# A fused attention and maxout-FFN kernel: token tiles grouped 2, 2, 4, 4, 4, 4, 4 in place of 4, 2, 2, 4, 4, 4, 4, with every engine's order of work written anew

## The chip, the cores and the metric

The kernel runs on one core of a Trainium2 chip. The metric is the device time of one execution in microseconds; the kernel before is given as the median of three runs. Beside it there is one profiled execution, whose trace gives every instruction's start and duration. The engines go by the profile's names: PE (matrix multiplications; PEld is its loading of weights), DVE (vector engine), ACT (activation engine), POOL (GpSimd) and SP (here the engine that issues nearly all DMAs).

## The reference

Causal attention with 8 global and 96 local keys, and a linear bias per head, over 4 batches, 8 heads, 768 positions of 64 dimensions. Its output, as 3072 tokens of 512 features, goes through a feed-forward layer whose hidden value is the maximum of three products.

```
scores = scale * (q @ k.T) - slope[h] * dist        # dist: i - j for local keys, 96 for global ones
a      = softmax(where(keep, scores, -1e9))          # keep: the 8 first keys, or 0 <= i - j < 96
x      = (a @ v) -> [3072, 512]
h      = max(max(x @ w1, x @ w2), x @ w3)            # [3072, 768]
out    = h @ w_out                                   # [3072, 512], float32
```

## The kernel before

**Tiles.** The 3072 tokens are 24 tiles of 128, six per batch. For a tile T the kernel multiplies its queries with the keys of the tile and of the tile before it, into whose first columns the global keys have been copied (`u_S`, on PE, two halves g of four heads each), takes the exponential (`u_e`, ACT), multiplies with a mask that holds the bias (`u_m`, DVE; a few tiles get the bias by a matmul, `u_b`, and no mask), multiplies with the values (`u_A`, PE) and normalises (`u_n`, DVE), which leaves the tile's 128x512 attention output `xb`. That is transposed to `xT`, by PE and a copy (`u_t`, `u_u`) or by a DMA transpose that SP issues (`u_Z`).

**Chunks.** The feed-forward layer works on chunks of tiles, by the list `SIZES`. A chunk of four tiles makes matmuls 512 columns wide, one of two tiles 256 wide. `u_F` makes a unit of hidden features: chunk c, block f of 128 of the 768 hidden features, product j of the three; four matmuls into one PSUM bank. `u_f` empties that bank: for j = 0 a copy by ACT or DVE into a buffer `h01`, for j = 1 a maximum on DVE into the same buffer, for j = 2 a maximum on DVE into `ht`. When all six blocks of a chunk are there, `u_O` multiplies with `w_out`, six matmuls to a tile, `u_o` copies the bank to `staging`, `u_s` writes it to memory.

**Loads.** SP issues all loads: q, k and v for pairs of tiles (group G is the tiles 2G and 2G + 1; `u_l`, 512 KB each; the first four tiles' q and k come as one quadruple, group 12), the three weights in two pieces each (`u_w`: blocks f = 0, 1, which are 512 KB, and blocks f = 2 to 5, which are 1 MB), and `w_out` in three pieces (`u_q`). What has landed is float32 and is cast to bfloat16 by ACT, DVE or POOL (`u_c`, `u_v`, `u_W`, `u_Q`); a cast on POOL is made in two halves. q and k of a pair are transposed to `qkT` by PE (`u_x`, `u_y`), or from tile 10 on by two DMA transposes (`u_X`). In weight casts `w123_0`, `w123_1`, `w123_2` hold the blocks f = 0, 1, f = 2, 3 and f = 4, 5 of all three weights.

**Order.** Nothing is scheduled by a program: the string `SCHEDULE` lists the units, and each engine runs its instructions in that order. A unit reads `F1.5.0@7`: function `u_F`, chunk 1, block 5, product 0, buffer slot 7 of its ring. `RINGS` gives the number of slots; for PSUM there are eight banks. An engine that waits holds up all that stands behind it in its list; an instruction that writes a slot waits until the slot's last reader is done. SP waits the same way: a load waits for its slot, a DMA transpose for the `xb` or the casts that it reads, and each DMA for the eighth before it.

**The end.** `u_E` makes the output of the last chunk: tiles 0 and 1, tile 2, then tile 3 in pieces of 256, 128 and 128 columns. After it the table has one tile that was kept back, tile 0 of chunk 5, whose output is stored in two halves.

Of the kernel before, what the change touches and what calls it, by code (L numbers as in the profile page):

```python
# [24 lines left out]
    l0.12.1@0 l1.12.1@1 D10.512@0 l1.12.3@2 l0.12.2@3 l0.12.3@4 R K7 K6 B1.1 K4 B2.1 K2 B3.0 K1 K5 B0.1 B6.1  # L25
    K0 c0.12.3.2@0 l1.12.2@5 c0.12.1.1 B4.1 B5.1 c1.12.1.1@1 K3 x12.0.1@0 y0.0.1.0@0 B7.1 l2.0.2@0 D3.256@1
    x12.1.1@1 b0.1@2 v1.0.2 l2.1.2@1 c1.12.3.1 v1.1.2 b1.0@4 y0.1.1.0 b1.1@6 S1.1.1 l0.2.2@6 c0.12.2.1
    y1.0.1.1@1 y1.1.1.0 x12.0.2@0 e1.1@0 c1.12.2.1 x12.0.3 y0.0.0.1 l1.2.2@0 y1.0.0.1 x12.1.3@1 x12.1.2
    y0.1.0.0 S0.1.1 e0.1@1 G0.1 b2.1@6 v2.0.2 v3.0.2 w1.0@0 S1.0.1 G1.0 e1.0@2 b2.0@2 w0.0@0 y1.1.0.1 S2.1.1
    w1.1@1 S0.0.0@0 e0.0@3 l2.2.2@2 S2.0.1 v0.0.1 e2.0@4 w0.1@1 v0.1.1 m0.0.1 e2.1@5 v2.1.2 b3.0@4 A1@0  # L30
    V1.1.1 V1.0.2 G2.1 v3.1.2 w0.2@2 A0@2 S3.0.1 e3.0@6 b3.1@6 n1@0 c0.2.2.2@2 S3.1.1 G3.0 A2@0 V2.0.2
    e3.1@7 V2.1.2 n0@1 t0@2 W0.0.2 c1.2.2.1 u0.0@0 x2.1.2@3 y2.1.2.0@2 w1.2@2 x2.0.2@2 A3@4 t1@6 u1.0 n2@2
    y2.0.2.1 t2@7 n3@3 l0.3.2@1 l1.3.2@2 S4.1.0@0 V3.1.2 e4.1@0 V3.0.2 S4.0.0@2 W1.1.2 u2.1 t3@6 G4.1 u3.0
    W2.0.1 S5.1.0@4 e5.1@2 S5.0.0@0 e5.0@1 m4.1.1 W1.0.1 e4.0@3 F0.5.0@7 F0.4.0@6 W2.1.0 F0.3.0@4 f0.3.0.0@0
    F0.2.0@5 f0.4.0.1@1 F0.1.0@6 v4.1.2 v4.0.2 l2.3.2@0 f0.1.0.0@2 q2@0 v5.1.0 F0.0.0@0 F0.5.1@1 F0.4.1@4
    F0.2.1@6 m4.0.1 f0.0.0.0@3 v5.0.0 f0.5.0.0@4 m5.1.1 A4@2 V4.1.0 F0.3.1@0 W0.1.2 f0.4.1.1 W0.2.0 m5.0.1
# [54 lines left out]

LAST_BANKS = (6, 7, 3, 0, 1, 4, 5, 2)

LAST_STAGES = (8, 2, 0, 10, 11, 7, 6, 3, 4, 9, 1, 5)


@with_exitstack
def kernel(
# [13 lines left out]
    nc = tc.nc  # L112
# [366 lines left out]
    def u_E(slot):  # L479
# [12 lines left out]
        for tt, p in enumerate(po):  # L492
            f2_mm(p, last, tt, range(NF - 1))
# [118 lines left out]
```

## Time and profile before

| | us |
|---|---|
| median of 3 runs | 176.49 |
| lowest and highest | 175.44 and 176.92 |
| profiled execution, span from the first to the last instruction | 174.8 |
| first feed-forward matmul starts | 21.58 |
| last matmul ends | 171.2 |

The page gives no time of its own for the profiled execution beside its span; the median of the runs lies 1.7 us above that span. A row of a group reads: line, engine, operation, what it writes from what it reads, sizes, count, then busy time, mean duration of one in ns, and the idle time before them with what ended it. Matmuls overlap in the array: a 512-column matmul is shown as lasting 379 ns but the next one starts after some 216 ns, so that the pace is read from the chain of waits, which gives a stretch of matmuls with its length and count.

### The profile page before, as it was taken

To read this page: it belongs to the slowest core of one execution; us is meant where nothing else is said; L and a number is where in the kernel's file an instruction comes from. 1 tells how busy PE (TensorE), PEld (TensorE's weight loads), DVE (VectorE), ACT (ScalarE), POOL (GpSimd) and SP (SyncE) were. 2 spreads that over 40 slices of the span, in tenths; PEclk is the share of its full clock that TensorE was granted. 3 is DMA by queue.
4 is the path that set the end of the run, shared out by engine and by line. 5 is a ranking of instruction groups with operands and counts; after the bars stand their busy time and mean duration, and the time that the engine had idled before them with its cause. 6 is when DMAs were issued, how large, how long until landed. Compare 5 with 4: busy or idle time off the path is not lost.

```text
span 174.8 us, 3865 instructions
## 1 busy us (share of the span) xinstructions
PE 165.9 (95%) x1485; PEld 93.6 (54%) x1507; DVE 131.9 (75%) x268; ACT 95.4 (55%) x147; POOL 54.7 (31%) x99
## 2 busy tenths in 40 slices
PE   7997999999999999898999999999999999999991
PEld 2555745577676877544445545544445554444460
DVE  7889864988599897989898678899578993074910
ACT  5988897672868788440667688200345651402051
POOL 4049295057586717003730003240530000000000
PEclk9999999999999999999999999999999999999998
DMA  5999999999899899999996759998990046370035
GB/s 149 352 292 327 402 360 385 270 371 311 229 303 179 139 183 266 267 290 284 165 135 112 114 145 306 305 210 260 231 213 20 0 120 137 121 286 4 0 119 185
DMA packets 66403, 37.36 MB, mean 214 GB/s; under 512 B 24144, under 2 KB 61392, under 8 KB 66384
## 3 DMA queue, kind: packets, MB, share of 16 engines
q1 hardware_dynamic: 66240, 37.04, 83.3%
q8 instruction: 12, 0.20, 0.5%
q10 hardware_dynamic: 144, 0.07, 0.1%
q14 instruction: 7, 0.06, 0.1%
HBM read 25.17 MB, written 6.29 MB: 180 GB/s over the span
## 4 chain that ended last, share of the span: by engine, by line
PE 76%; DVE 10%; DMA 6%; ACT 3%; issue 2%; SPq 0%; DVEq 0%
PE psum L433 44%; PE psum L457 17%; PE psum L349 6%; DMA xT<-xb 3%; DMA rawqk<-in_k_dram 3%; DVE P L365 3%; PE psum L391 3%; PE psum L394 2%; PE psum L276 2%; DVE ht L452 1%; DVE xb L403 1%; ACT P L356 1%; PE psum L270 1%; DVE qb L195 1%; PE psum L335 1%
## 5 line engine op out<-in xcount | busy, mean ns | idle before, releaser
L433 PE MATMUL psum<-xT,w 128*128 128x512 bf16 (+1 forms) x491 | 97.5, 348 | 1.5 <-DMA xT<-xb 0.7
L433 PEld LDWEIGHTS <-w 128*128 128x128 bf16 x504 | 47.6, 98 | 42.9 <-DMA xT<-xb 0.9
L356 ACT ACTIVATE P<-psum 128x1024 bf16<-128x1024 f32 (+1 forms) x48 | 43.3, 954 | 10.4 <-PE psum L349 10.3
L449 DVE TENSOR_TENSOR h<-h,psum 128x512 bf16<-128x512 bf16 (+1 forms) x42 | 25.0, 605 | 15.9 <-PE psum L433 12.4
L457 PE MATMUL psum<-wo,ht 128*128 128x512 bf16 (+2 forms) x147 | 33.4, 362 | 0.5
L447 ACT CAST h<-psum 128x512 bf16<-128x512 f32 (+1 forms) x27 | 13.8, 523 | 33.1 <-PE psum L433 29.8
L452 DVE TENSOR_TENSOR ht<-h,psum 128x512 bf16<-128x512 bf16 (+1 forms) x42 | 26.2, 644 | 2.1 <-PE psum L433 0.9
L365 DVE TENSOR_TENSOR P<-P,wmask 128x1024 bf16<-128x1024 bf16 x34 | 25.2, 752 | 2.0 <-ACT P L356 1.7
L457 PEld LDWEIGHTS <-ht 128*128 128x128 bf16 x156 | 13.8, 98 | 13.5 <-DVE ht L452 0.2
L254 POOL CAST va<-rawv 64x512 bf16<-64x512 f32 x28 | 18.5, 668 | 4.8 <-DMA rawv<-in_v_dram 3.7
L323 POOL COPY va<-vaf 4x260 int32<-4x260 int32 x17 | 7.2, 424 | 34.9 <-PE psum L394 34.5
L403 DVE TENSOR_TENSOR xb<-psum,rz 128x512 bf16<-128x512 f32 x24 | 16.6, 692 | 0.8
L201 POOL CAST qb<-rawk 128x512 bf16<-128x512 f32 x12 | 7.5, 654 | 23.7 <-DMA rawk<-in_k_dram 23.7
L349 PE MATMUL psum<-qkT 64*128 64x128 bf16 x352 | 14.4, 217 | 0.5 <-DVE qkT L315 0.4
L391 PEld LDWEIGHTS <-P 128*128 128x128 bf16 x192 | 12.6, 97 | 3.2 <-ACT P L356 0.4
L349 PEld LDWEIGHTS <-qkT 64*128 64x128 bf16 x352 | 10.0, 94 | 7.9 <-issue 5.9
L391 PE MATMUL psum<-va,P 128*128 128x65 bf16 x160 | 12.7, 193 | 0.7 <-DVE ht L452 0.6
L447 DVE CAST h<-psum 128x512 bf16<-128x512 f32 (+1 forms) x15 | 9.1, 615 | 5.1 <-PE psum L433 5.1
L471 ACT COPY staging<-psum 128x512 f32<-128x512 f32 x14 | 8.2, 592 | 8.8 <-PE psum L457 8.8
L201 POOL CAST qb<-rawq 128x512 bf16<-128x512 f32 x14 | 8.9, 664 | 9.0 <-DMA rawq<-in_q_dram 5.0
L394 PEld LDWEIGHTS <-P 128*128 128x128 bf16 x160 | 10.5, 97 | 2.1 <-issue 0.7
L394 PE MATMUL psum<-va,P 128*128 128x65 bf16 x128 | 9.9, 193 | 0.0
(72 smaller groups left out, 120.6 us busy)
## 6 DMA issues: line engine op xcount, KB each, us to landing
rawv<-in_v_dram SPq DMA_DIRECT2D x12, 512.0 KB, 7.0
out_dram<-staging SPq DMA_DIRECT2D x21, 256.0 KB, 2.7
rawq<-in_q_dram SPq DMA_DIRECT2D x10, 512.0 KB, 7.1
rawk<-in_k_dram SPq DMA_DIRECT2D x10, 512.0 KB, 7.3
staging<-in_moe_w_dram SPq DMA_DIRECT2D x3, 1024.0 KB, 9.3
staging<-in_moe_w_dram SPq DMA_DIRECT2D x3, 512.0 KB, 8.8
staging<-in_moe_w_out_dram SPq DMA_DIRECT2D x3, 512.0 KB, 6.3
out_dram<-staging SPq DMA_DIRECT2D x5, 128.0 KB, 2.2
```

Source lines behind the costliest of these rows:

```text
L254: copies[how](heads(va(T))[64 * e:64 * e + 64, :, 0:D], src)
L349: nc.tensor.matmul(sp[:, hh, j2, ds], qT(T - ds, 1, hsl, jp), qT(T, 0, hsl, jp), start=not how, stop=True, skip_group_check=True)
L356: nc.scalar.activation(P[:, :, 0:n], sps[T, g].rearrange("p a b d n -> p (a b) d n")[:, :, 0:n], AF.Exp, bias=0.0, scale=scale)
L365: mul(P, P, wmask[:, g, :, 0:2])
L391: nc.tensor.matmul(o, P[:, i, 0], heads(va(T))[:, h], start=True, stop=(t == 0), skip_group_check=True)
L394: nc.tensor.matmul(o, P[:, i, 1], heads(va(T - 1))[:, h], start=False, stop=True, skip_group_check=True)
L403: nc.vector.tensor_tensor(out=x.rearrange("p (g h) d -> p g h d", g=2), in0=o4[:, :, :, 0:64], in1=rz[:, :, :, None].to_broadcast([128, 2, ...
L433: nc.tensor.matmul(ps, w123[f // 2][:, j, dm, (f % 2) * 128:(f % 2) * 128 + 128], xT[c][:, dm], start=(dm == 0), stop=(dm == 3))
L447: copies[how](h01, ps)
L449: nc.vector.tensor_max(h01s[c, f], h01s[c, f], ps)
L452: nc.vector.tensor_max(dst, h01s[c, f].rearrange("p (t e i) -> p t e i", e=2, i=64), ps.rearrange("p (t e i) -> p t e i", e=2, i=64))
L457: nc.tensor.matmul(po, ht[c][:, f, tt * 128:(tt + 1) * 128], wo[:, f, cols], start=(f == 0), stop=(f == NF - 1))
```

## The change

- `SIZES` becomes 2, 2, 4, 4, 4, 4, 4. Chunks 0 and 1 are now tiles 0 and 1, and tiles 2 and 3; before, tiles 0 to 3 were one chunk and the two chunks of two tiles came after it. Chunk 2 is now tiles 4 to 7. The number of matmuls of each width is the same.
- `SCHEDULE` is another list throughout. Among its units, seven tiles (not nine) are transposed by PE and 17 (not 15) by DMA; the dummy matmuls that stand between the first units (`u_D`) are one piece of one and three pieces of two, not one piece of three; ACT takes 13 copies of global values rather than 4, and 15 casts of values rather than 6, mostly from POOL.
- `RINGS`: 9 slots for `h01` (not 5), 6 for raw q and k (not 7), 3 for `qkT` (not 4).
- `u_E`, `f2_mm`, `f2_out`, `LAST_BANKS` and `LAST_STAGES` are gone. `u_O`, `u_o` and `u_s` take ranges instead (hidden blocks, and columns in steps of 64), and the last chunk is listed like the others. Its tile 3 is made in parts of 128, 256 and 128 columns; the last 128 columns are the last work of the program.

```diff
-SIZES = [4, 2, 2, 4, 4, 4, 4]
-RINGS = {'r': 7, 'rv': 3, 'qb': 3, 'qkT': 4, ..., 'h01': 5, 'rz': 4, 'os': 12}
-LAST_BANKS = (6, 7, 3, 0, 1, 4, 5, 2)
-LAST_STAGES = (8, 2, 0, 10, 11, 7, 6, 3, 4, 9, 1, 5)
+SIZES = [2, 2, 4, 4, 4, 4, 4]
+RINGS = {'r': 6, 'rv': 3, 'qb': 3, 'qkT': 3, ..., 'h01': 9, 'rz': 4, 'os': 12}
 SCHEDULE = """
...
-    F6.5.0@1 f6.5.0.1@2 F6.5.2@5 f6.5.1.1 f6.5.2.1 E@7 O5.0@2 o5.0.0@5 s5.0.2
+    s6.1 s6.2 s6.3.6.8 s4.3 o5.2.0@4 s5.2 O6.0.0.5.0.8@5 O6.0.5.6.0.8 o6.0.1@0 s6.0 O5.0@4 o5.0.0@2 s5.0
+    O6.3.0.6.0.4@5 o6.3.0.4.1@7 s6.3.0.4 O6.3.0.6.4.6@0 o6.3.4.6.0@9 s6.3.4.6
...
-    def u_O(slot, c, tt):
-        pos[c, tt] = ring("h", slot, [128, DM], FP32, "po")
-        f2_mm(pos[c, tt], c, tt, range(NF))
+    def u_O(slot, c, tt, f0=0, f1=NF, c0=0, c1=8):
+        if slot is not None:
+            pos[c, tt, c0] = ring("h", slot, [128, (c1 - c0) * 64], FP32, "po")
+        for f in range(f0, f1):
+            nc.tensor.matmul(pos[c, tt, c0], ht[c][:, f, tt * 128:(tt + 1) * 128], wo[:, f, c0 * 64:c1 * 64],
+                             start=(f == 0), stop=(f == NF - 1))
...
-    def u_E(slot):
...
+    def u_s(slot, c, tt, c0=0, c1=8, queue=0):
         T = chunks[c][tt]
...
+        (nc.sync, nc.scalar)[queue].dma_start(out=out[T * 128:(T + 1) * 128, c0 * 64:c1 * 64], in_=osts[c, tt, c0])
```

What this moves is seen engine by engine. First SP's list from k of group 2 (tiles 4, 5) on: before, then now. `moe_w1` to `moe_w3` are the three weights, 4x512 the 1 MB piece and 4x256 the 512 KB piece.

```order
L236 DMA rawk_250<-in_k_dram 128x8x128
L514 DMA staging_92<-in_moe_w1_dram 128x4x512
L514 DMA staging_92<-in_moe_w1_dram 128x4x256
L514 DMA staging_92<-in_moe_w2_dram 128x4x512
L236 DMA rawv_304<-in_v_dram 128x8x128
L514 DMA staging_92<-in_moe_w2_dram 128x4x256
L514 DMA staging_92<-in_moe_w3_dram 128x4x256
L514 DMA staging_92<-in_moe_w3_dram 128x4x512
L236 DMA rawq_468<-in_q_dram 128x8x128
```

```order
L229 DMA rawk_218<-in_k_dram 128x8x128
L472 DMA staging_92<-in_moe_w1_dram 128x4x512
L472 DMA staging_92<-in_moe_w1_dram 128x4x256
L229 DMA rawv_223<-in_v_dram 128x8x128
L472 DMA staging_92<-in_moe_w2_dram 128x4x512
L481 DMA staging_92<-in_moe_w_out_dram 128x2x512
L472 DMA staging_92<-in_moe_w2_dram 128x4x256
L472 DMA staging_92<-in_moe_w3_dram 128x4x256
L472 DMA staging_92<-in_moe_w3_dram 128x4x512
L229 DMA rawk_548<-in_k_dram 128x8x128
```

The values of tiles 4 and 5 (`rawv_304`, now `rawv_223`) went ahead of the large piece of w2, and a first piece of `w_out`, which stood behind q, k and v of tiles 6 and 7, went ahead of the small piece of w2. The weights stood ahead of q and k of tiles 6 and 7 before, too.

Second, POOL's list around the weight casts: before, then now. `va` are values with their column of ones, `vaf` those of a batch's first tile, and a copy of 4x260 puts the global values in.

```order
L323 COPY va1_101<-vaf0_106 4x260 x2
L201 COPY w123_0_110<-staging_92 128x512 x2
L323 COPY va2_102<-vaf0_106 4x260 x2
L201 COPY w123_1_111<-staging_92 128x512 x2
L254 COPY va3_103<-rawv_304 64x8x64 x2
L201 COPY w123_0_110<-staging_92 128x512 x2
```

```order
L316 COPY va1_101<-vaf0_106 4x260
L194 COPY w123_2_112<-staging_92 128x512 x2
L247 COPY va4_104<-rawv_223 64x8x64
L316 COPY va2_102<-vaf0_106 4x260
L194 COPY w123_0_110<-staging_92 128x512 x6
L194 COPY qb_570<-rawk_566 128x512 x2
```

POOL casts w1's blocks 4, 5 (DVE did), and all three weights' blocks 0, 1 in a row; ahead of those three stands a cast of the values of tile 5, `rawv_223`.

Third, SP's list from the last load of group 5 (tiles 10, 11) on: before, then now.

```order
L236 DMA rawk_835<-in_k_dram 128x8x128
L236 DMA rawv_852<-in_v_dram 128x8x128
L236 DMA rawq_919<-in_q_dram 128x8x128
L236 DMA rawv_947<-in_v_dram 128x8x128
L292 DMA_TRANSPOSE qkT_1090<-qb_811 128x16x64 x2
L292 DMA_TRANSPOSE qkT_1115<-qb_841 128x16x64 x2
```

```order
L229 DMA rawk_640<-in_k_dram 128x8x128
L417 DMA_TRANSPOSE xT_680<-xb_658 128x4x128
L417 DMA_TRANSPOSE xT_680<-xb_721 128x4x128
L229 DMA rawv_780<-in_v_dram 128x8x128
L285 DMA_TRANSPOSE qkT_924<-qb_687 128x16x64
L229 DMA rawv_933<-in_v_dram 128x8x128
L285 DMA_TRANSPOSE qkT_924<-qb_687 128x16x64
L229 DMA rawk_981<-in_k_dram 128x8x128
L229 DMA rawq_1022<-in_q_dram 128x8x128
L229 DMA rawq_1070<-in_q_dram 128x8x128
L417 DMA_TRANSPOSE xT_1072<-xb_1066 128x4x128
```

`qb_811` and `qb_841` are the cast q and k of groups 5 and 6 in the kernel before, `qb_687` those of group 5 now. Before, all of q and k up to group 6 was issued ahead of the first of these transposes; now q and k of group 6 (`rawk_981`, `rawq_1022`) stand behind the transposes of group 5, and so behind the cast of `rawk_640` that they wait for.

165 lines of the change are left out of this document (64 added, 101 removed).

## Prediction

> **What bounds the kernel now.** I read the page's head first, then busy times by stretches of the span, then the chain of waits and PE's own waits.
>
> ```profile
> span 174.8 us, 3865 instructions
> PE 165.9 (95%) x1485; PEld 93.6 (54%) x1507; DVE 131.9 (75%) x268; ACT 95.4 (55%) x147; POOL 54.7 (31%) x99
> ```
>
> ```profile
> 0.00:21.60 21.60, 18.90 (x236) 11.18 (x237) 18.37 (x54) 17.98 (x31) 9.12 (x22) 1.00 1.01 303
> 21.60:45.80 24.20, 23.98 (x197) 14.71 (x201) 17.84 (x34) 16.15 (x24) 14.75 (x25) 1.00 1.06 330
> 45.80:69.00 23.20, 22.99 (x292) 16.68 (x297) 20.22 (x44) 18.56 (x30) 13.54 (x23) 1.00 1.06 213
> 69.00:90.00 21.00, 19.54 (x150) 10.58 (x151) 18.07 (x35) 8.94 (x13) 6.55 (x12) 1.00 1.11 237
> 90.00:135.00 45.00, 44.52 (x375) 22.60 (x381) 36.65 (x67) 21.97 (x33) 9.94 (x19) 1.00 0.85 192
> ```
>
> In the stretches the columns are length, then busy time of PE, PE's weight load, DVE, ACT and POOL, granted clock, share of the DMA engines, GB/s. From 21.6 us on PE lacks 0.2 us in a stretch, but for 69 to 90, where it lacks 1.46; up to 90 us the DMA engines are full as well.
>
> ```profile
> 21.58 0.38 PE psum L433
> 58.27 2.18 PE psum L433 x20
> 60.45 0.55 PE psum L349 x16
> 67.78 4.98 DMA xT<-xb
> 155.42 9.23 PE psum L433 x42
> ```
>
> ```profile
> PE psum L433 <- DMA xT<-xb: 0.7, 1, 0.7
> PE psum L391 <- DVE ht L452: 0.6, 1, 0.6
> ```
>
> The chain (start, length, what) gives PE's pace: 9.23/42 = 0.220 us for a matmul of 512 columns, 2.18/20 = 0.109 for 256, 0.55/16 = 0.034 for a score matmul. The first feed-forward matmul is at 21.58. The two waits of PE are those of the stretch 69 to 90: one for a DMA transpose that was issued at 67.78 and took 4.98, one for DVE. So PE bounds all but the first 21.6 us, about 1.2 us in the middle (1.46 less the usual 0.2), and the last 3.6 us.
>
> **The change part by part.** I sum against the profiled execution, 174.8 us; the median of the runs is 1.7 above it.
>
> *PE's work* is unchanged. Both tables have 90 units of 512 columns and 36 of 256, and the output parts add up alike; two tiles fewer transposed on PE (eight matmuls of 128 columns) are made up by four dummy matmuls more of 256. Counted at these paces, 15.7 us of work stand ahead of the first feed-forward unit now, 15.8 before. All that can change is waiting.
>
> *The first feed-forward unit.* Its weights, w1's blocks 4 and 5, went from DVE to POOL.
>
> ```profile
> 20.51 0.69 DVE L195 CAST w<-staging 128x1024 bf16<-128x1024 f32 x1
> 21.75 1.67 POOL L201 CAST w<-staging 128x512 bf16<-128x512 f32 x2 [3.20 <-DMA staging<-in_moe_w_dram]
> 24.34 2.17 POOL L201 CAST w<-staging 128x512 bf16<-128x512 f32 x2
> 27.80 1.17 POOL L201 CAST w<-staging 128x512 bf16<-128x512 f32 x2
> 24.33 1.71 DVE L365 TENSOR_TENSOR P<-P,wmask 128x1024 bf16<-128x1024 bf16 x2
> ```
>
> The loads up to there keep their order, so the piece has landed by 20.51 as before; DVE took 0.69 for it, POOL takes 1.17 to 2.17, and is done at 21.7 to 22.7. Half of the unit's matmuls wait for the second half only. Against that, the exponentials and copies ahead of the unit are dealt out anew and may end 0.3 earlier. I take +0.3 (-0.3 to +0.9).
>
> The three POOL rows are the same work. The slowest coincides with two mask multiplications on DVE, whose operands both lie in SBUF. The Trainium skill (SBUF — State Buffer, section "Who interferes with whom") says that a DVE instruction with two SBUF inputs and a GpSimd instruction that reads SBUF exclude each other for a whole instruction. By that rule a cast that meets two masks would take 1.17 + 1.71 = 2.9, and the next step 0.7 more than by the row; the trace shows 2.17, so part of the blocking falls on DVE or doesn't happen, and I keep the rows.
>
> *The weights of blocks 0 and 1.* Ahead of them POOL now has the cast of tile 5's values and a copy.
>
> ```profile
> 13.73 0.83 SPq L514 DMA_DIRECT2D staging<-in_moe_w_dram  x1
> staging<-in_moe_w_dram SPq DMA_DIRECT2D x1, 1024.0 KB, 10.5
> 14.61 1.35 SPq L236 DMA_DIRECT2D rawv<-in_v_dram  x1
> rawv<-in_v_dram SPq DMA_DIRECT2D x1, 512.0 KB, 11.1
> 16.01 4.67 SPq L514 DMA_DIRECT2D staging<-in_moe_w_dram  x1
> staging<-in_moe_w_dram SPq DMA_DIRECT2D x1, 512.0 KB, 11.3
> ...
> L254 POOL CAST va<-rawv 64x512 bf16<-64x512 f32 x28 | 18.5, 668 | 4.8 <-DMA rawv<-in_v_dram 3.7
> L323 POOL COPY va<-vaf 4x260 int32<-4x260 int32 x17 | 7.2, 424 | 34.9 <-PE psum L394 34.5
> ```
>
> Issue plus time to landing: w2's 1 MB at 13.73 + 10.5 = 24.2, tile 5's values at 25.7, w2's 512 KB at 27.3. The DMA engines are full, so each load costs the distance to the one ahead: 2.5 for 1 MB (POOL's row shows the piece ahead landed at 21.75), 1.5 and 1.6 for 512 KB. Now the values stand right behind that piece and land at 21.75 + 1.5 = 23.25. POOL adds 0.67, 0.42 and the cast's 1.67: w1's blocks 0, 1 are ready at 26.0 (25.5 to 26.5). PE wants them six units of 256 columns and 16 score matmuls after its first unit: 21.9 + 6 x 4 x 0.109 + 16 x 0.034 = 25.1, or 25.3 for the half that comes last: it waits 0.7. w2's blocks 0, 1 land at 23.25 + 2.5 + 1.5 (the piece of w_out put ahead) + 1.6 = 28.85 and are cast by 30.5; PE, 4.0 us of work later, wants them at 30.0: 0.5 more. w3's are cast 1.67 after that, and wanted 1.7 after that. Together +1.2 (0.4 to 2.0).
>
> *DVE in the woven chunks.* All 36 narrow units now lie between the first unit and chunk 2.
>
> ```profile
> L449 DVE TENSOR_TENSOR h<-h,psum 128x256 bf16<-128x256 bf16 x12 | 5.0, 416 | 2.5 <-PE psum L433 1.8 <-ACT h L447 0.7
> L452 DVE TENSOR_TENSOR ht<-h,psum 128x256 bf16<-128x256 bf16 x12 | 5.1, 441 | 0.4 <-PE psum L433 0.2
> L365 DVE TENSOR_TENSOR P<-P,wmask 128x1024 bf16<-128x1024 bf16 x34 | 25.2, 752 | 2.0 <-ACT P L356 1.7
> L403 DVE TENSOR_TENSOR xb<-psum,rz 128x512 bf16<-128x512 f32 x24 | 16.6, 692 | 0.8
> ```
>
> In that stretch PE has 27.5 us of work. DVE has 24 maxima (12 x 0.416 + 12 x 0.441 = 10.3), ten masks (at most 7.5), four normalisations (2.8), three weight casts and four casts and copies of q and k (7 x 0.69 = 4.8) and a dozen small ones (about 3): 28.4, less some overlap of neighbours. So DVE is full for 27 us where before it was busy 17.84 of 24.2, and banks come back late; but PE's waits for weights give it time to catch up: +0.1 (0 to 0.8).
>
> *The middle.* The two waits of 69 to 90 (1.2) go if the last transpose of chunk 3 (tiles 8 to 11) comes in time. It is SP's queue that decides.
>
> ```profile
> 50.23 2.34 POOL L201 CAST qb<-rawk 128x512 bf16<-128x512 f32 x4 [0.41 <-DMA rawk<-in_k_dram]
> 51.49 8.85 SPq L292 DMA_TRANSPOSE qkT<-qb  x4
> 65.45 3.55 SPq L424 DMA_TRANSPOSE xT<-xb  x2
> qkT<-qb SPq DMA_TRANSPOSE x4, 4.7
> rawq<-in_q_dram SPq DMA_DIRECT2D x2, 512.0 KB, 6.1
> ```
>
> Group 5's k landed at 50.23; one 512 KB load fewer (1.6) stands ahead of it now: 48.6, cast by 49.9. From there SP issues a transpose (8.85/4 = 2.2), v, the second transpose, then group 6's k and q (0.6 each): q out at 55.5, landed 6.1 later, cast by 62.9. Then two transposes for group 6, tile 9's (3.55/2 = 1.8), one for group 7, and tile 10's, issued at 62.9 + 3 x 2.2 + 1.8 = 71.3, or at 67.1 if each takes half that, landed 4.98 later: 72.1 to 76.3. PE wants it at 72.0 (72.76 less the wait of 0.7), less 0.8 because less work stands ahead, plus the 1.6 lost so far: 72.8. I take a wait of 0.6, near the lower end, because the loads are fewer by then; and 0.4 further on, where DVE again has more than PE between chunk 3's last units. Against the 1.2 saved: -0.2 (-1.2 to +2.7).
>
> *The tail.*
>
> ```profile
> 166.21 4.96 PE psum L457 x34
> 171.19 0.58 ACT L471 COPY staging<-psum 128x512 f32<-128x512 f32 x1 [1.03 <-PE psum L457]
> 171.80 0.81 SPq L477 DMA_DIRECT2D out_dram<-staging  x2
> ...
> L462 ACT COPY staging<-psum 128x128 f32<-128x128 f32 x1 | 0.3, 265 | 0.3 <-PE psum L457 0.3
> ```
>
> After the last matmul (171.17) came a 512-column copy of 0.58 and two stores. Now it is a 128-column copy of 0.27 and one store, issued when those of the other parts are out: 0.3 less for the copy, up to 0.4 for the issue, but SP has two stores to issue just ahead. I take -0.4 (-0.7 to 0).
>
> Sum: 0.3 + 1.2 + 0.1 - 0.2 - 0.4 = +1.0: the median of 176.49 becomes 177.5. A difference under 1% (1.8 us) I count as no change.
>
> **The rivals.**
>
> *Slower: SP's queue holds chunk 3.* At the upper end tile 10's transpose lands at 76.3 and PE stands 3.5 rather than 0.6: 177.5 + 2.9 = 180.4. It decides once that landing is later than 74.2 (72.8 + 0.6, and the 0.8 that lead from 177.5 to 1% over). For it: the four transposes from 51.49 on were that slow beside loads, and group 6's loads now wait behind group 5's casts. Against it: PE's own late start moves the need back, and after 50 us fewer loads crowd the queue. Chance 0.30; a further 0.10 goes to the upper ends of the start (178.8).
>
> *Faster: everything comes in time.* POOL's casts take 1.17, the first unit starts 0.3 earlier, banks come back in time, both waits of the middle and 0.7 of the tail go: -0.3 + 0.4 + 0 - 1.2 - 0.7 = -1.8, 174.7, and less if the landing times gain too. For it: in the middle the chunk's last attention product is about 1 us of PE work further ahead of its use. Against it: POOL's order and the full DMA engines are facts of the table and of the trace. Chance 0.17.
>
> *The queue was not what it is called.* That weights go ahead of q and k of tiles 6, 7 was so before; only a piece of w_out is new there, and its 1.5 us are in the sum. No chance of its own.
>
> **How the numbers follow.** The forecast, a change within 1%, most likely on its slow side, has 0.43 (175 to 178.2); slower by more has 0.30 + 0.10 = 0.40; faster by more 0.17. The time is 177.5. For 8 in 10 the range goes from 174.4, a little under the fast case with 0.12 left below, to 180.4, the slow case, with 0.08 above.
>
> **What would show it.** The first feed-forward unit at 21.3 to 22.2, with its third matmul held by POOL; the first unit of block 0 held by a POOL cast that ends near 26; DVE without gaps from 24 to 50; a wait of PE for tile 10's transpose near 73; a last store issued within 0.6 of the last matmul. I am wrong if PE's total of waits between 22 and 45 us stays under 0.4, or if PE stands more than 1.5 us in one place.

## The result and the profile after

| | before | after |
|---|---|---|
| median of four runs each, us | 176.27 | 182.84 |
| ratio, with its 95% interval | | 1.0369 (1.0328 to 1.0409) |
| span of the profiled execution | 174.8 | 181.2 |
| first feed-forward matmul | 21.58 | 23.38 |
| last matmul ends | 171.16 | 176.90 |

The change costs 6.6 us; one of its four runs, of 185.15 us, was in a slower state than the others and is left out of the ratio (the other three have 182.60 in the middle). First the head of the page of the changed kernel, then its stretches (columns as before: length, busy time of PE, PE's weight load, DVE, ACT, POOL, granted clock, DMA share, GB/s).

```profile
span 181.2 us, 3857 instructions
PE 166.9 (92%) x1485; PEld 92.9 (51%) x1503; DVE 135.0 (75%) x265; ACT 103.3 (57%) x159; POOL 50.1 (28%) x88
```

```profile
0.00:23.40 23.40, 18.00 (x224) 10.61 (x225) 15.81 (x50) 17.91 (x30) 10.36 (x26) 1.00 1.00 303
23.40:40.00 16.60, 15.51 (x175) 13.23 (x174) 16.33 (x35) 12.76 (x22) 5.97 (x9) 1.00 1.09 334
40.00:56.50 16.50, 15.15 (x170) 9.54 (x171) 14.69 (x30) 11.14 (x16) 9.50 (x14) 1.00 1.03 229
56.50:90.00 33.50, 32.31 (x296) 16.73 (x299) 26.14 (x47) 22.32 (x31) 12.52 (x19) 1.00 1.04 218
90.00:135.00 45.00, 44.30 (x387) 22.85 (x393) 36.47 (x66) 29.20 (x46) 11.39 (x21) 1.00 0.89 180
```

PE has the same work (165.9 us busy then, 166.9 now), and the granted clock is 1.00 in every stretch, so everything lost is waiting. To see where, I counted the work that PE's list puts ahead of an instruction, at the paces that the prediction read from the chain, and took that from the instruction's start; what is left is PE's lag there.

| lag of PE, us | before | after | lost in between |
|---|---|---|---|
| first feed-forward matmul | 5.7 | 7.7 | 1.9 |
| attention product of tile 9 (52 to 55 us of work) | 6.4 | 12.5 | 4.2 |
| that of tile 13 (75 us of work) | 7.9 | 13.1 | -1.0 |
| last matmul | 9.4 | 15.1 | 0.6 |
| end of the span | 13.0 | 19.4 | 0.6 |

So 1.9 us go at the start, 4.2 in the stretch where the narrow chunks are woven with the attention of tiles 4 to 9, 0.6 after the last matmul, and the middle gains 0.4 (-1.0 and +0.6). PE's own waits of the changed kernel say on whom it waited (in total, times, longest).

```profile
PE psum L426 <- DVE h L442: 2.0, 3, 0.9
...
PE psum L328 <- ACT bias L366: 0.9, 1, 0.9
PE psum L342 <- ACT qkT L276: 0.8, 1, 0.8
PE psum L384 <- DVE P L360: 0.7, 1, 0.7
PE psum L490 <- DVE qkT L276: 0.6, 1, 0.6
```

L328 is a bias matmul and L276 a copy of transposed q and k: the start. L442 (a maximum that empties a bank) and L360 (a mask) are DVE's: 0.6 and 0.7 us of them lie in the stretch, 1.4 at 62.9 and 89 us. The view shows each wait too short, since it counts idle time alone and a 512-column matmul's row lasts 0.16 us longer than its pace, and it leaves out short ones; by the distances of the starts the stretch has nine waits over 0.15 us, 3.9 in all. Seven of the nine end with an instruction of DVE, none with a cast of weights or a DMA transpose.

Stretches with the same busy time of PE show what became of it. Before, then after:

```profile
21.60:52.40 30.80, 30.53 (x267) 19.49 (x271) 22.92 (x46) 21.46 (x31) 18.88 (x31) 1.00 1.06 319
```

```profile
23.40:56.50 33.10, 30.66 (x343) 22.77 (x344) 31.02 (x63) 23.91 (x37) 15.48 (x22) 1.00 1.06 281
```

Beside 30.6 us of busy PE (by its list 30.6 us of work before, but 28.8 now, since the rows hide short waits) DVE now spends 31.0 us, not 22.9: two more masks, one more normalisation, three more weight casts, two casts of q, and copies of kept keys and values, some of them far longer than their size. Two rows of DVE and POOL in the changed kernel (start, length, count at the end):

```profile
24.27 1.48 DVE L308 COPY qkT<-kg 128x32 bf16<-128x32 bf16 x1
25.78 0.29 DVE L318 COPY va<-vaf 4x520 bf16<-4x520 bf16 x1
```

```profile
23.86 0.74 POOL L316 COPY va<-vaf 4x260 int32<-4x260 int32 x1
24.55 1.16 POOL L194 CAST w<-staging 128x512 bf16<-128x512 f32 x2
```

A copy of 32 columns, 0.15 to 0.18 us where no instruction of POOL overlaps it, takes 1.48 us and ends when POOL's casts do. So there were two readings of the stretch: DVE has too much to do, or POOL blocks it; and a third from the forecast, that weights and loads hold PE.

### The profile page after: what moved, and what is told of

The parts are those of the page before. It is cut to its first block, busy times and chain, and to the rows that moved or that the text cites. A ratio compares the mean times of both kernels' runs of the same rounds, so it can differ in the third digit from the quotient of the medians.

```text
span 181.2 us, 3857 instructions
## 1 busy us (share of the span) xinstructions
PE 166.9 (92%) x1485; PEld 92.9 (51%) x1503; DVE 135.0 (75%) x265; ACT 103.3 (57%) x159; POOL 50.1 (28%) x88
## 4 chain that ended last, share of the span: by engine, by line
PE 69%; DVE 18%; ACT 6%; issue 3%; DMA 2%; SPq 1%; DVEq 0%; ACTq 0%
PE psum L426 44%; PE psum L453 12%; PE psum L342 5%; DVE P L358 4%; PE psum L384 3%; PE psum L387 2%; DVE xb L396 2%; DMA out_dram<-staging 2%; DVE h L442 2%; ACT P L349 2%; ACT wmask L371 1%; DVE qkT L276 1%; PE psum L269 1%; ACT qkT L276 1%; DVE qkT L308 1%
## 5 line engine op out<-in xcount | busy, mean ns | idle before, releaser
L426 PE MATMUL psum<-xT,w 128*128 128x512 bf16 (+1 forms) x492 | 99.2, 348 | 2.9 <-DVE h L442 2.0
L349 ACT ACTIVATE P<-psum 128x1024 bf16<-128x1024 f32 (+1 forms) x48 | 43.9, 953 | 13.1 <-PE psum L342 11.9
L453 PE MATMUL psum<-wo,ht 128*128 128x512 bf16 (+2 forms) x150 | 33.1, 362 | 0.5 <-issue 0.2
L442 DVE TENSOR_TENSOR h<-h,psum 128x512 bf16<-128x512 bf16 (+1 forms) x42 | 24.6, 602 | 8.3 <-PE psum L426 4.2
L358 DVE TENSOR_TENSOR P<-P,wmask 128x1024 bf16<-128x1024 bf16 x34 | 26.6, 793 | 5.3 <-ACT P L349 5.2
L445 DVE TENSOR_TENSOR ht<-h,psum 128x512 bf16<-128x512 bf16 (+1 forms) x42 | 25.6, 640 | 1.3 <-PE psum L426 0.3
L440 ACT CAST h<-psum 128x512 bf16<-128x512 f32 (+1 forms) x28 | 13.5, 509 | 22.4 <-PE psum L426 22.2
L459 ACT COPY staging<-psum 128x512 f32<-128x512 f32 (+1 forms) x18 | 9.8, 551 | 24.8 <-PE psum L453 23.1
L247 POOL CAST va<-rawv 64x512 bf16<-64x512 f32 x20 | 13.5, 674 | 17.0 <-DMA rawv<-in_v_dram 9.8
L384 PE MATMUL psum<-va,P 128*128 128x65 bf16 x160 | 12.6, 193 | 0.2 <-DVE xb L396 0.2
L316 POOL COPY va<-vaf 4x260 int32<-4x260 int32 x12 | 6.0, 500 | 24.3 <-PE psum L387 11.5
L194 POOL CAST qb<-rawq 128x512 bf16<-128x512 f32 x10 | 7.0, 729 | 17.3 <-DMA rawq<-in_q_dram 13.5
L318 ACT COPY va<-vaf 4x520 bf16<-4x520 bf16 x13 | 8.1, 621 | 5.9 <-PE psum L387 5.8
```

The costliest lines, as they stand in the source:

```text
L194: copies[how](dst[s], src[s])
L349: nc.scalar.activation(P[:, :, 0:n], sps[T, g].rearrange("p a b d n -> p (a b) d n")[:, :, 0:n], AF.Exp, bias=0.0, scale=scale)
L358: mul(P, P, wmask[:, g, :, 0:2])
L384: nc.tensor.matmul(o, P[:, i, 0], heads(va(T))[:, h], start=True, stop=(t == 0), skip_group_check=True)
L426: nc.tensor.matmul(ps, w123[f // 2][:, j, dm, (f % 2) * 128:(f % 2) * 128 + 128], xT[c][:, dm], start=(dm == 0), stop=(dm == 3))
L440: copies[how](h01, ps)
```

## The experiments

The theory to test had three parts: the start is lost by PE's list and by copies that wait for one another; the stretch by DVE; the tail by stores. Rivals: loads and weights, the narrow units as such, POOL. The time of a single variant is known to some 0.7 to 1.3 us (the half width of the intervals is 0.4 to 0.8%, and 0.2% for `before_tail` with its 12 runs), so small steps are read from the traces. These vary as well: `tail_slots`, which edits nothing ahead of the last two copies, starts its feed-forward matmuls with the changed kernel (23.39) and reaches tile 9's attention product 0.9 us sooner; `moved_copies` starts them 0.8 later with nothing edited ahead of them. Only four variants differ clearly in time from what they were made of: `weights_sooner`, `all_parts`, `before_dve` and `before_tail`.

**The start: bias matmul later.**

```diff
-... b0.1@0 c1.12.2.2 x12.0.1@2 ... w1.1@1 b1.1@4
+... c1.12.2.2 x12.0.1@2 ... w1.1@1 b0.1@0 b1.1@4
```

> The changed kernel with one unit moved in the list: tile 0's bias matmul goes behind the last transposes of the first group of k, where PE no longer waits for ACT's bias ahead of the transposes. Theory (the start: PE's list puts a matmul that waits for ACT ahead of the transposes, and all copies behind them are late): PE's 0.9 us wait at 5 us goes, the first scores come 1.0 to 1.3 us sooner, the first feed-forward matmul at about 22.1 to 22.4 instead of 23.38, time -1.0 to -1.6 us (181.2 to 181.8). Rival A (VectorE full from 23 to 56 us is the only limit there): the start gains but the stretch gives it back, time -0.3 to 0. Rival B (the order of copies on ACT sets the first scores): first scores within 0.3 of 12.89, time unchanged.

Measured 181.73 us, ratio to the kernel before 1.0301 (1.0239 to 1.0362), 1.1 less than the changed kernel. PE's wait for the bias is gone, but scores and first feed-forward matmul come only 0.57 us sooner (12.32, 22.81), half of what was expected: now POOL's casts of k are what PE waits for. The surprise is behind it. At tile 9's attention product the lag is 2.8 us less than in the changed kernel, 2.2 of them won in the stretch (1.3 against `tail_slots`), and DVE's order there reads:

```profile
22.84 0.68 DVE L187 CAST w<-staging 128x1024 bf16<-128x1024 f32 x1
23.43 0.17 DVE L307 COPY qkT<-kg 128x32 bf16<-128x32 bf16 x1
23.63 0.61 DVE L317 COPY va<-vaf 4x520 bf16<-4x520 bf16 x1
24.27 0.42 DVE L439 CAST h<-psum 128x256 bf16<-128x256 f32 x1
```

```profile
24.50 1.16 POOL L193 CAST w<-staging 128x512 bf16<-128x512 f32 x2
```

(Line numbers are one less in this variant.) POOL's weight cast comes at the same time as before, since a landing sets it; DVE, 0.57 us sooner, slips its two copies in ahead of it, and the 32 columns take 0.17 us. One us of what was won goes again later, most of it in a wait of 0.70 at 111 us for a copy that POOL makes.

**The start: copies too.** Besides the above, group 1's first k half is copied by DVE and group 0's by ACT, and group 1's first q half (the text below calls it a k half) goes ahead of group 0's.

```diff
-... y1.1.0.0 y0.1.0.1 ... y0.0.0.1 ... y1.0.0.1
+... y1.1.0.1 y0.1.0.0 ... y1.0.0.1 y0.0.0.1
```

> The changed kernel with the bias matmul moved as in the first run, and besides at the start the copy of group 1's first k half on VectorE and that of group 0's on ACT, not the other way, and group 1's second k half ahead of group 0's. Theory (VectorE's copies stood 1.6 to 2.2 us idle behind ACT's copy of the other half of the same PSUM tile): the first scores of group 1's second half come at 11.5 to 11.8 instead of 12.89 (12.3 in the first run), the first feed-forward matmul at 22.2 to 22.5, and the time is 0.3 to 0.8 us under that of the first run (181.0 to 181.4). Rival (another chain, the values and attention of tiles 0 and 1, sets the start): the first feed-forward matmul within 0.2 of the first run's 22.81, time as there.

Measured 183.00 us, 1.0377 (1.0332 to 1.0421). The scores in question come at 12.21, only 0.1 sooner than in the run before, the first feed-forward matmul at 22.48; and the time isn't better for it. The gain is gone by 100 us, in waits that were not there: 0.95 for a feed-forward copy of ACT at 36, 0.73 at 48 and 0.65 at 96 for POOL's values, 0.69 for a DMA transpose at 76, 1.08 for POOL's copy at 114. The rival stands: other engines have set their own times behind the start.

**The stretch: less work for DVE.** The masks of tiles 4 to 7 are left out (`m4.0.1` to `m7.1.1`).

> The changed kernel without the mask multiplications of tiles 4 to 7 (eight instructions of VectorE, 6.7 us by their mean of 842 ns): these tiles' attention weights are left unmasked. Theory (VectorE is full from 23 to 56 us and PE's banks come back late): the 4.0 us that PE loses between its first feed-forward unit and 56 us mostly go, time -2.8 to -4.0 us (178.8 to 180.0), the start unchanged. Rival A (weights behind the values in the queues hold PE, as forecast): PE's feed-forward units of blocks 0 and 1 still wait, time -0.5 to 0. Rival B (narrow units as such, each with its fixed costs, hold PE): -1.0 to -2.0.

Measured 182.50 us, 1.0349 (1.0304 to 1.0394). In the stretch the theory is right in the main: the lag at tile 9's attention product is 2.8 us less than in the changed kernel (1.9 less than in `tail_slots`), and of PE's waits that the view shows between 23.4 and 56.5 us one of 0.3 is left. But 1.5 us are lost again: a wait for a DMA transpose at 74, for POOL's values at 94 and for POOL's copy at 111, each behind a PE that is now earlier. The time is the changed kernel's.

**The stretch: weights sooner.** Two loads go back in SP's list.

```diff
-... l2.2.2@2 w1.1@1 ... q0@1 w0.1@2 ... w0.2@0 ... w1.2@0
+... w1.1@1 ... w0.1@2 l2.2.2@2 ... w0.2@0 ... w1.2@0 q0@1
```

> The changed kernel with two loads put later in SP's queue: the values of tiles 4 and 5 go behind the second piece of w2, and the first piece of w_out behind the last piece of w3, so that the weights of w2 and w3 land 1.5 to 3 us sooner. Theory (VectorE is the limit): time within 0.5 us of the changed kernel's 182.8. Rival (the forecast's term: weights of blocks 0 and 1 hold PE): time -0.8 to -2.0 us.

Measured 186.67 us, 1.0593 (1.0552 to 1.0635): 3.8 slower, which neither had. Some 0.8 of it is lost by the first feed-forward matmul (24.21). PE's waits between 23 and 45 us in this variant:

```profile
PE psum L425 <- POOL w L193: 2.0, 2, 1.8
PE psum L386 <- ACT va L317: 1.4, 1, 1.4
```

The weights are loaded sooner, but POOL's list has the cast of tile 5's values ahead of theirs; it waits for the values, and PE for the weights behind it. That the change loads the values first is not what costs; it is what the order of POOL's casts needs.

**The stretch: one copy, then two, away from POOL's cast.**

The first line is the edit of the first variant, the second has both.

```diff
-G4.1
+G4.0
-V3.1.1
+V3.1.0
```

> The changed kernel with one copy of 128 x 32 elements (the kept keys of tile 4) on ACT instead of VectorE. On VectorE it took 1.48 us at 24.27, beside GpSimd's casts, while its like takes 0.17 to 0.22 elsewhere. Theory (GpSimd's casts, which read and write SBUF, hold up VectorE's instructions that do the same): VectorE runs 1.3 us ahead from there, PE's waits between 25 and 33 us (0.32, 0.44, 0.80, 0.22) mostly go, the second feed-forward chunk's scores come 1 us sooner, time -0.8 to -1.8 us (181.0 to 182.0). Rival (it is VectorE's amount of work alone): its next instruction takes up the blocking, time -0.3 to 0.

> The changed kernel with two copies from SBUF to SBUF on ACT instead of VectorE: the kept keys of tile 4, and the kept values of tile 3, which stood next in VectorE's order and took 1.49 us instead of 0.27 once the first was gone. The instruction behind them reads PSUM. Theory (GpSimd's cast of a weight from 24.6 to 25.7 blocks whichever VectorE instruction works on SBUF alone, and no other): VectorE's first cast of a feed-forward result starts at 24.5 to 24.9 instead of 26.10, the scores of tile 5 are unchanged or sooner, PE's waits from 25 to 33 us fall from 1.8 to at most 0.7, time -0.8 to -1.5 us (181.3 to 182.0). Rival (VectorE's amount of work decides, blocked or not): its casts start sooner, but the waits come back before 36 us, time -0.3 to 0.

Measured 182.38 us, 1.0356 (1.0288 to 1.0424), and 182.22, 1.0337 (1.0291 to 1.0383). With the first copy gone, DVE and POOL read:

```profile
24.53 1.49 DVE L318 COPY va<-vaf 4x520 bf16<-4x520 bf16 x1
26.05 0.42 DVE L440 CAST h<-psum 128x256 bf16<-128x256 f32 x1
```

```profile
24.01 0.74 POOL L316 COPY va<-vaf 4x260 int32<-4x260 int32 x1
24.71 1.16 POOL L194 CAST w<-staging 128x512 bf16<-128x512 f32 x2
```

The next copy from SBUF to SBUF takes the blocking, to the same end: it goes from 0.29 to 1.49. So POOL's work blocks whichever of these copies meets it, and taking away the one that suffered passes that on: the time of the first run is nearer to its rival's. With both copies away DVE's first feed-forward cast starts at 24.47, as expected, rather than at 26.10, but PE's waits between 25 and 33 us fall only from 1.8 to 1.4, now partly for ACT, which has the copies. The expected 0.8 to 1.5 us are not shown.

**The stretch: four pieces from DVE to ACT.**

```diff
-W2.2.1 ... G6.1 ... c0.4.2.1 ... v7.0.1
+W2.2.0 ... G6.0 ... c0.4.2.0 ... v7.0.0
```

> The changed kernel with four pieces of VectorE's work between 36 and 49 us on ACT: the cast of w3's blocks 4, 5 (0.68 us), of group 4's q (0.68), of tile 7's values (0.42) and the copy of tile 6's kept keys (0.61). Theory (VectorE has too much to do there): of PE's waits between 46 and 53 us (0.34, 0.26, 0.84, 0.54) 1.2 to 1.8 us go, and the time falls by 0.8 to 1.8 us (181.0 to 182.0). Rival (PE waits there for exponentials and masks of tiles 6 to 8 as they follow one another, whatever else VectorE does, and ACT, with 1.0 us more each, sends them later): time 0 to +0.8.

Measured 183.16 us, 1.0398 (1.0361 to 1.0435). The rival: a wait of 1.34 for ACT's cast of q at 42.5 and one of 0.60 for its copy of values at 35.4 take the place of DVE's. ACT is no spare engine there. A later start (24.16) and a wait of 1.06 for DVE's cast of a weight at 25 lie ahead of the edit.

**The stretch: wide units.** Chunks 0 and 1 are one chunk of four tiles, each wide unit where the first of its halves stood.

```diff
-SIZES = [2, 2, 4, 4, 4, 4, 4]
+SIZES = [4, 4, 4, 4, 4, 4]
```

> The changed kernel with its first two chunks of 2 tiles made one chunk of 4, so six chunks of 4: each unit stands where the first of its two halves stood. 24 narrow maxima (0.41 and 0.44 us) become 12 wide ones (0.68 and 0.72), which takes 1.8 us off VectorE, 6 copies off ACT, and leaves PE's work as it is. Theory (VectorE's load in the woven stretch): of the 4.0 us lost there 1.0 to 2.0 come back, time -0.8 to -2.0 us (180.8 to 182.0). Rival A (two narrow chunks at the front are the loss as such): -3 to -4.5 us (178.3 to 179.8). Rival B (a wide unit needs its weights and frees its bank later): 0 to +1.5.

Measured 182.58 us, 1.0361 (1.0314 to 1.0408). No gain; PE stands 1.69 us at 37.6 for DVE's cast of a weight, 0.98 at 40 for a maximum of DVE, and 1.27 at 46.8 for an exponential. So the run doesn't bear out that the narrow chunks at the front are the loss as such (rival A would be 178.3 to 179.8); with an order that was made for another list, it doesn't rule it out either.

**The stretch, from the other side: load DVE in the kernel before.** Eleven pieces go from ACT to DVE; PE's list is untouched.

```diff
-W2.1.0 W0.2.0 W1.2.0 W2.2.0 c0.3.2.0 v5.1.0 v5.0.0 y3.0.2.0 y4.1.2.0@0 y4.0.2.0 o0.2.0@0
+W2.1.1 W0.2.1 W1.2.1 W2.2.1 c0.3.2.1 v5.1.1 v5.0.1 y3.0.2.1 y4.1.2.1@0 y4.0.2.1 o0.2.1@0
```

> The kernel before with eleven pieces of ACT's work from 24 to 51 us on VectorE, as the change dealt out such pieces: four casts of weights, one of q, two of values, three copies of transposed q and k, one of an output tile (7.0 us at VectorE's own lengths). VectorE was busy 24 us of the 29 from 21.5 to 50.5; now it would have 31. Theory (the amount given to VectorE in that stretch is the loss of 4 us): PE gets waits for VectorE's feed-forward maxima between 24 and 52 us of 1.5 to 3.5 us in all, time +1.2 to +3.5 us against the kernel before. Rival (VectorE's amount does no harm as long as chunk 0 is wide and GpSimd doesn't block it): -0.3 to +0.5.

Measured 180.96 us, 1.0275 (1.0199 to 1.0351): 4.8 us slower. The first feed-forward matmul is where it was (+0.06), tile 9's attention product 4.5 later, and the last matmul 4.6 later. PE's waits there, and the stretch with nearly the same PE work as before:

```profile
PE psum L457 <- DVE h L449: 1.3, 1, 1.3
PE psum L433 <- DVE h L449: 0.6, 2, 0.4
PE psum L349 <- DVE qkT L287: 0.5, 1, 0.5
PE psum L433 <- DVE h L447: 0.4, 1, 0.4
```

```profile
21.60:57.00 35.40, 31.92 (x282) 19.84 (x283) 30.56 (x57) 12.60 (x21) 24.41 (x38) 1.00 1.13 302
```

DVE's 30.6 us beside 31.9 of busy PE are about what the changed kernel has there (31.0 beside 30.7), and the loss is the same. Chunk 0 is wide in this kernel, and PE's list and the loads are as they were, so small work dealt to DVE is enough to lose 4 us. Whether it is its amount or where the pieces stand isn't separated: the loss was above the range I had expected, though DVE isn't even full (86%). A part, the first wait of 0.5 at 24.9, is by the chain of waits DVE itself waiting for a weight's landing with the bank's copy behind it.

**All parts together.** The bias matmul moved, both copies and tile 16's copy of kept keys on ACT, and the stores sooner (below).

> The changed kernel with the bias matmul moved, the two copies on ACT, the later kept-keys copy of tile 16 (1.05 us of PE's time where PE is earlier) on ACT, and the stores put sooner. If the parts add up: -2.5 to -3.5 us (179.3 to 180.3). Rival (each gain is taken by the next piece that is late: GpSimd's casts of values, the landings of q and k): -1.0 to -1.7 us (181.1 to 181.8).

Measured 180.20 us, 1.0247 (1.0200 to 1.0295): 2.6 us better than the changed kernel. That is what I expected if the parts add up, though hardly one of them showed by itself. By the traces it is not the two copies that add much: at tile 9's attention product all parts are 0.2 us sooner than the bias matmul alone, and 0.9 more come between tiles 13 and 17, where three waits of `head_bias`, 2.1 us in all, become 1.3. The stretch, with the same PE work as above:

```profile
23.00:53.80 30.80, 30.39 (x347) 22.89 (x344) 26.87 (x61) 24.61 (x39) 13.53 (x22) 1.00 1.09 290
```

DVE spends 26.9 us, not 31.0, beside the same work. The two copies that left it took 1.8 of the 4.1. The rest is the same instructions taking less; in groups of the stretch, the changed kernel and then this one:

```profile
L358 DVE TENSOR_TENSOR P<-P,wmask 128x1024 bf16<-128x1024 bf16 x8 | 6.7, 842 | 0.0
...
L188 DVE CAST w<-staging 128x1024 bf16<-128x1024 f32 x4 | 3.3, 853 | 0.0
L396 DVE TENSOR_TENSOR xb<-psum,rz 128x512 bf16<-128x512 f32 x4 | 2.8, 691 | 0.1
L360 DVE TENSOR_TENSOR P<-P,wmask 128x512 bf16<-128x512 bf16 x2 | 1.7, 827 | 0.0
```

```profile
L358 DVE TENSOR_TENSOR P<-P,wmask 128x1024 bf16<-128x1024 bf16 x8 | 6.0, 756 | 0.8 <-ACT P L349 0.8
...
L396 DVE TENSOR_TENSOR xb<-psum,rz 128x512 bf16<-128x512 f32 x4 | 2.8, 691 | 0.1
L188 DVE CAST w<-staging 128x1024 bf16<-128x1024 f32 x4 | 2.6, 681 | 0.0
...
L360 DVE TENSOR_TENSOR P<-P,wmask 128x512 bf16<-128x512 bf16 x2 | 0.8, 416 | 0.0
```

Masks and casts of weights, which work in SBUF, go from 842 to 756, from 853 to 681 and from 827 to 416 ns; the normalisation, which reads PSUM, stays at 691. They meet POOL less: these ten masks and four casts overlap its instructions for 7.8 us in the changed kernel and for 2.0 in this one.

**On top of that, the masks, and the start.** `all_fewer_masks` leaves the masks out again; `all_head` also makes the first cast of k on DVE (`c1.12.1.1@0`) and the copies of q and k as in `head_copies`.

> The kernel of the run with all parts, without the mask multiplications of tiles 4 to 7 (left unmasked). Theory (with the start 0.4 sooner and the blocked copies gone VectorE is no longer what PE waits for in the stretch): time within 0.5 us of that run (179.7 to 180.7). Rival (VectorE's amount still holds the stretch): -0.8 to -1.5 us (178.7 to 179.4).

> The kernel of the run with all parts, and besides at the start the first cast of the first group's k on VectorE, as in the kernel before, not on GpSimd, and the order of copies of the earlier run. Theory (the rest of the start, 1.4 us, is GpSimd's slow casts and the copies that wait for one another): the first feed-forward matmul comes at 21.8 to 22.4 instead of 23.0, time -0.4 to -1.2 us against that run (179.0 to 179.8). Rival (what follows is then held by loads and by GpSimd's casts of values, as in the run with the copies alone): the first feed-forward matmul as early, time -0.2 to +0.5.

Measured 181.37 us, 1.0313 (1.0267 to 1.0358), and 181.91, 1.0314 (1.0255 to 1.0372). Neither gains; both lie above both of their ranges. Without masks PE stands 0.74 us for a DMA transpose at 73.9 and 0.79 for DVE at 87. The start of `all_head` comes 0.5 sooner still (22.53), short of the 21.8 to 22.4, and the last matmul 0.7 later than in `all_parts`. What is left of the loss, 4 us, is thus not DVE's amount alone, and a start that is sooner does not come out at the end.

**The stretch over the runs.** From the first feed-forward matmul to tile 9's attention product: what PE lost (the time less the work of its list), DVE's busy time, and how much longer DVE's instructions on SBUF were than the mean of their like that no instruction of POOL overlaps in these runs.

| us | lost | DVE busy | longer beside POOL |
|---|---|---|---|
| kernel before | 0.4 | 31.0 | 1.8 |
| `before_dve` | 4.9 | 37.5 | 2.4 |
| changed kernel | 4.8 | 37.4 | 5.6 |
| `tail_slots` (nothing edited here) | 3.9 | 36.4 | 4.4 |
| `two_copies` | 3.8 | 34.9 | 3.2 |
| `moved_copies` | 4.4 | 33.2 | 2.9 |
| `head_bias` | 2.6 | 34.5 | 2.5 |
| `fewer_masks` | 2.0 | 30.6 | 2.8 |
| `all_parts` | 2.2 | 33.0 | 1.4 |
| `all_fewer_masks` | 2.4 | 29.0 | 1.4 |

PE's work by its list is 39.4 us in the first two rows and 36.4 in the others. The first three rows and `fewer_masks` speak for DVE's load, by more than the 0.9 that come without an edit. The rest says that it isn't all: `all_fewer_masks` has 4 us less of DVE than `all_parts` and loses no less, and `moved_copies` has DVE's time of `all_parts` and twice its loss. In every variant of the changed kernel here at least 2.0 us are lost, of which the kernel before has 0.4; what holds them isn't shown.

**The tail: slots, then stores.**

Both variants have the new slots, the second one also the stores.

```diff
-o6.3.0.4.1@7 ... o6.3.4.6.0@9
+o6.3.0.4.1@6 ... o6.3.4.6.0@11
-s2.0 ... o4.2.1@5 ... s2.3 ... s4.2 ... s4.0 s3.1 ... s4.3
+s2.0 s4.0 s4.3 s3.1 s2.3 ... o4.2.1@5 s4.2
```

> The changed kernel with the last two staging buffers chosen anew: the last part of the last tile goes to slot 11 and the 256-column part to slot 6, whose stores ended long before, instead of 9 and 7. Theory (the tail: the last copy waits 1.47 us for a store that was issued only 4 us earlier): the copy starts about 0.1 to 0.3 us after the last matmul, the last store lands 0.7 to 1.2 us sooner, time -0.7 to -1.2 us (181.6 to 182.1). Rival (SP's issue of the stores ahead, or the stores themselves, set the end): the copy is early but the last store is issued within 0.3 of where it was, time -0.3 to 0.

> The changed kernel with the staging slots of the earlier run and five stores, whose data were long ready, further up in SP's list: ahead of the last chunk's feed-forward units instead of among the last 13 stores, which keep the DMA engines at some 400 GB/s from 168 us to the end. Theory (the tail is set by the draining of 3.4 MB of stores, not by the slot): from the last matmul to the end it takes 2.6 to 3.2 us instead of 4.27, time -1.1 to -1.7 us (181.1 to 181.7). Rival (SP's issues, 0.4 to 0.65 us each behind one another's copies, set the end): -0.3 to 0.

In the changed kernel the last copy waited for the store that had last used its slot:

```profile
176.66 0.42 DVE L459 COPY staging<-psum 128x256 f32<-128x256 f32 x1 [1.31 <-ACT staging L459]
178.05 0.27 ACT L459 COPY staging<-psum 128x128 f32<-128x128 f32 x1 [1.47 <-DMA out_dram<-staging]
```

With other slots the copy starts 0.03 us after the last matmul (176.62):

```profile
176.65 0.27 ACT L458 COPY staging<-psum 128x128 f32<-128x128 f32 x1 [0.36 <-PE psum L452]
```

But from the last matmul to the end it takes 4.27 us as before (median 182.56, 1.0360, 1.0319 to 1.0400): the rival. With five stores sooner it takes 4.08 (181.97, 1.0339, 1.0291 to 1.0386); the time is 0.9 less, but 0.8 of that is won before the last matmul, in a stretch that the edit doesn't touch. That tail was between 3.1 and 4.8 us in the variants that share its slots, so its 0.6 us stay unexplained.

**The tail in the kernel before.** The one output tile that stood last goes ahead of the part that ends in 128 columns.

```diff
-E@7 O5.0@2 o5.0.0@5 s5.0.2
+O5.0@2 o5.0.0@5 s5.0.2 E@7
```

> The kernel before with one thing of the change: the ordinary output tile that stood last goes ahead of the part that ends in 128 columns, so that the last copy is of 128 columns and the last store goes by ACT's queue. Theory (the forecast's term for the tail: a shorter copy and one store to issue): time -0.4 us (-0.7 to 0) against the kernel before. Rival (the end is set by the landing of the stores, 2.0 to 2.9 us from issue whatever their size): within 0.2 us.

Measured 175.29 us over 12 runs, ratio 0.9946 (0.9926 to 0.9966): 0.9 us faster than the kernel before, a little more than expected, and the fastest of all. From the last matmul to the end it takes 3.34 us, not 3.67. Most of the other 0.6 of the two profiled executions is the wait for a DMA transpose at 72 us, which this one doesn't have though nothing was edited there; so the gain of the edit itself lies between 0.3 by the trace and 0.6 to 1.3 by the times.

## Why the prediction was wrong

It said 177.5, no change, with 180.4 as the slow end; it is 182.84. The terms of its sum:

*PE's work unchanged*: right, 161.8 us of it by the paces in both.

*First feed-forward unit, +0.3 (-0.3 to +0.9)*: mis-sized, measured +1.9. The term looked at the cast of w1's last blocks, which was as said: POOL made it in 1.16 us from 20.43, and it held nobody. "The exponentials and copies ahead of the unit are dealt out anew and may end 0.3 earlier" is the smaller of two steps that failed: I took what is dealt out anew as neutral without following it. PE's list had a bias matmul ahead of the first transposes, and copies of one PSUM tile were split over two engines, which in these rows run one after the other. The rows of the changed kernel, first PE, then the two copying engines behind it:

```profile
6.55 0.38 PE L328 MATMUL psum<-bias,identb 128*128 128x256 bf16 x2 [0.92 <-ACT bias L366]
7.42 0.69 DVE L276 COPY qkT<-psum 128x512 bf16<-128x512 bf16 x1 [1.60 <-PE psum L263]
8.14 1.56 ACT L276 COPY qkT<-psum 128x512 bf16<-128x512 bf16 x3 [1.23 <-DVE qkT L276]
11.55 1.89 DVE L276 COPY qkT<-psum 128x512 bf16<-128x512 bf16 x3 [2.15 <-ACT qkT L276]
```

The runs recovered 0.6 of the 1.9 by the bias matmul and 0.9 by both; a cast of k put back on DVE, on top of the other parts, did not bring the rest, which stays open.

*Weights of blocks 0 and 1, +1.2*: not there. The landings were right, as POOL's rows show (forecast 23.25 for the values, 28.85 for w2's blocks):

```profile
23.18 0.61 POOL L247 CAST va<-rawv 64x512 bf16<-64x512 f32 x1 [1.58 <-DMA rawv<-in_v_dram]
28.17 3.58 POOL L194 CAST w<-staging 128x512 bf16<-128x512 f32 x4 [2.45 <-DMA staging<-in_moe_w_dram]
```

But PE came later than the weights. The mechanism exists, as `weights_sooner` shows with a wait of 2.0 us for it.

*DVE in the woven chunks, +0.1 (0 to 0.8)*: this is the larger step that failed, by 4 us. The count was right: 28.4 us of DVE work beside 27.5 of PE's (31.0 beside 30.7 by the rows above), "DVE is full for 27 us where before it was busy 17.84 of 24.2, and banks come back late". What failed is what followed, "PE's waits for weights give it time to catch up": the cover was a wait that didn't come, and the price without it was not set. Nor were the durations safe: I took casts and copies at 0.69, their length with no POOL instruction beside them, and masks at 752 ns, where the changed kernel's stretch has 853 for weight casts and 842 for masks. Loading DVE in the kernel before with 7 us of small pieces cost 4.8 us with PE's list and the loads unchanged; taking masks away gave 1.9 to 2.8 back in the stretch.

On the blocking the Trainium skill (SBUF — State Buffer, section "Who interferes with whom") says that a DVE copy or cast in a two-port mode and GpSimd lock each other out for whole instructions, and that a DVE instruction with at most one SBUF input outside these modes is free of it. The traces agree in kind: 0.17 us becomes 1.48 beside POOL, though no single POOL instruction there lasts longer than 0.74, while the normalisation, whose only SBUF input is a small table, takes 0.69 with POOL beside it or not. In the prediction I had weighed that rule for POOL's casts only, and not for what DVE would lose.

*The middle, -0.2*: right in size, -0.4, and in part by luck: the wait of 0.6 that it holds didn't come, and DVE held a unit of chunk 3 for 1.1 us at 89, where I had 0.4. Tile 10's transpose was issued at 72.14 (forecast 67.1 to 71.3) and landed at 74.6, within the 72.1 to 76.3; the chunk that needs it began at 77.78, as PE was late itself.

```profile
72.14 1.20 SPq L417 DMA_TRANSPOSE xT<-xb  x1
77.78 4.42 PE psum L426 x20
```

So the rival that I gave 0.30 did not come, at least not behind a PE that comes 5 us later than the 72.8 of the forecast. Where PE is earlier it does wait for DMA transposes there, for q and k of tile 14 (0.62 in `fewer_masks`, 0.69 in `head_copies`, 0.74 in `all_fewer_masks`). Of the 0.40 for slower by more, 0.30 stood on this queue and 0.10 on the start; the start did come, beyond its upper end, and the larger part came by a cause that I had at 0.1 us.

*The tail, -0.4*: wrong sign, +0.6. Alone, in the kernel before, the step has the sign and about the size that I gave it. In the changed kernel it comes with 15 stores in the last 13 us and the slot above; why the tail is longer there isn't settled.

Of the signs that I had named, DVE's stretch came, nearly without gaps (31.0 of 33.1 us). The first unit at 21.3 to 22.2, its third matmul held by POOL, block 0 held by a cast and the wait near 73 did not, and the last store was issued 1.44 us after the last matmul, not 0.6. Neither sign of being wrong came (PE's waits between 22 and 45 us were over 0.4, and none over 1.5 in one place): they were set for weights and the queue, and did not ask on whom PE waits.

Of the sum, then, 1.9 and 4.2 are the start and the stretch. In the stretch DVE's load, POOL's blocking included, is shown for some 2 to 3 us of the 4.2; how the two share them isn't settled, since one moves the other, and the rest is open; what the narrow units at the front cost by themselves was not tested apart. Open is also why `all_parts` is still 4.0 us slower than the kernel before: in the profiled executions 3.4, of which 1.5 lie at the start, 1.8 in the stretch and 0.5 in the tail, with 0.4 gained between.

## What to carry to other kernels

Where an engine beside the critical one goes from three quarters full to full in a stretch, count that as a likely loss on the critical path unless you can name a row that covers it; a cover that is itself a forecast wait is none. Read the order of each engine up to the first big stretch unit by unit when everything is dealt out anew, since one matmul that waits for a small operand in front of the list delays all that follows. In a kernel where several engines are near full, remove losses together and judge the sum: a single repair can be taken by the next engine's own due time. And before a difference of two traces is read as the work of an edit, look at a variant that edits nothing in that stretch: here such a pair differed by 0.9 us.

## What the runs showed of the hardware

A DVE copy within SBUF that meets POOL can be held over several of POOL's instructions in a row. The copy of 32 columns starts at 24.27, inside POOL's copy that runs to 24.60, and ends at 25.75, when the two casts behind that copy are done (25.71); it didn't get in between. The one that took its place in `one_copy` did the same (24.53 to 26.02, POOL's casts to 25.87).

With a start 0.57 us sooner, `head_bias` reached tile 9's attention product 2.2 us sooner still, while DVE's instructions were 2.5 us longer beside POOL there and not 5.6. That which instruction meets which makes the difference fits, but isn't shown: 0.9 of such a gain came in `tail_slots` without an edit there. The runs of `head_bias` lie between 179.96 and 182.66, 2.7 us apart; those of the kernel before 1.5.
